# Decoding float64 weights in two steps with the low word rounded on ScalarE, and eleven joint units

## The chip, the cores and the metric

The kernel runs on one core of a Trainium2 chip. The metric is the device time of one execution in microseconds; lower is better. It is compared as the median of several executions. A core has five engines with queues of their own: PE (TensorE, matmul), DVE (VectorE), ACT (ScalarE), POOL (GpSimd) and SP (SyncE, which here issues all the DMAs).

## The reference

Chunked attention with memory tokens, and behind it a mixer with a low-rank token part and a feed-forward part. Batch 4, 8 heads, 768 tokens, head size 64; the model width is 512, the hidden width 2048, the rank 32.

```python
for c in range(nc):                      # chunks of 32 tokens, context 16 left, 8 right, 8 memory tokens
    scores = scale * np.matmul(q_c, k_full.transpose(0, 1, 3, 2))
    a = np.exp(scores - np.max(scores, axis=-1, keepdims=True))
    a = a / (np.sum(a, axis=-1, keepdims=True) + 1e-09)
    out[:, :, c_start:c_end] = np.matmul(a, v_full)
...
h = x.transpose(0, 2, 1) @ U @ V
u = x + h.transpose(0, 2, 1)
ch = np.maximum(u @ w_ch1, 0.0) @ w_ch2
return (u + ch).astype(np.float32)
```

U, V, w_ch1 and w_ch2 come as float64 (the random draws are scaled by a float64 factor), so each weight is two 32-bit words in memory. The kernel has to make numbers of them on the chip.

## The kernel before, in words

**Decoding.** A weight's upper word (sign, exponent, 20 bits of fraction) and lower word lie side by side. The class `Words` (L174) works on a chunk of 128 partitions x 512 numbers, each in three methods and a beginning. `begin` (L189, the instruction is recorded at L194) has ScalarE multiply the upper word, read as a float32, by 2^-112, which shifts the exponent to its place after the next step. `bits` (L199) has VectorE shift the result left by three (L201) and put the sign back (L202): that is the float32 of the upper 20 bits, its last three bits zero. `low` (L206) masks out the exponent (L208) and multiplies it by the lower word and 2^-52 (L211), both on VectorE. `join` (L216, L218) adds the two as floats. A chunk has one raw piece or two, and `begin` and `low` issue one instruction for each piece. Three pairs of work tiles rotate for the chunks in flight (`work_pair`, L156).

**High and low parts.** TensorE multiplies in a reduced precision form of float32, so each product is made of three: high x high, high x low, low x high. `finish` (L313) makes the parts of a chunk: ScalarE casts the joined value to the high part (L330), VectorE subtracts that from it (L331). Low parts of w_ch1 (`w1l`) are saved to HBM (L311) and fetched again for later passes (L379).

**The stream.** w_ch1 and w_ch2 are 16 slices f of 128 hidden columns, so 32 chunks (even ones of w_ch1, odd ones of w_ch2). `stream` (L340) is a generator that decodes them in order, three steps a chunk: in the first the bits of chunk n (and the beginning of chunk n + 1 and the finish of chunk n - 1), in the second its low word, in the third its join. `advance(k)` takes k steps. Whoever needs slice f runs the stream until `done` has reached 2f + 2. `more_w` (L867) issues the loads of raw words five slices ahead.

**The order of the work.** The attention of batch 0 comes first; a few steps of the stream are set into its end (L761, L766, L770). Then `both_blocks` (L1020) does the feed-forward part of batch 0 while the weights are still being decoded. A block is 384 tokens, a batch has two. A unit is one slice f for one block: `w1_step` (L950, matmuls at L958, 12 of them; then ScalarE's relu L964 and VectorE's low part L965) and `w2_step` (L978, matmuls at L1006 and L1011). For f below SPLIT the units of both blocks alternate ("joint"), so that each decoded slice serves two units; from SPLIT on come the solo units of block 0 (f = SPLIT to 15), then those of block 1. Units are counted by n. In each unit the stream is advanced by RATE steps behind its `w1_step`. From n = 2 x SPLIT - 6 the loads of batch 1's attention begin, and behind n = 2 x SPLIT one piece of that attention (`border`, L1082) stands ahead of each unit's `w1_step` and one behind it; what is left over is done in the last unit (L1063). The pieces are short stretches such as the turning of keys (L501), scores (L558), the reduction and the exponentials (L584, L587), transposes (L620), products with the values (L635). The values of tile 1 go to the buffer that tile 0 used (`v_home`, L454), those of tile 2 into a buffer that serves as decoding workspace before. Batches 1 to 3 then run block by block.

The engines' orders: TensorE and SyncE go by the order of the program throughout. VectorE does so up to n = 2 x SPLIT (`paced.close`, L1040) and ScalarE up to n = 2 (`head.close`, L1037); behind those points a planner with modelled costs sets their orders when the program is built. An engine executes its list strictly in order.

Of the kernel before, what the change touches and what calls it, by code (L numbers as in the profile page):

```python
# [9 lines left out]
F32R = mybir.dt.float32r  # L10
BF16 = mybir.dt.bfloat16
AF = mybir.ActivationFunctionType
ALU = mybir.AluOpType
AX = mybir.AxisListType
PSUM = bass.MemoryType.PSUM
I32 = mybir.dt.int32
U32 = mybir.dt.uint32
# [3 lines left out]
NVE = 1  # L21
# [10 lines left out]
WLO = 4  # L32
HIGH = 400
LEAD = 1
SPLIT = 10
EARLY = 5
NDEC = 3
RATE = 3
AHEAD = 2
SOON = 6  # L40
RATEL = 3
# [4 lines left out]
def chunk_attn_then_mixer_kernel(  # L46
# [13 lines left out]
    nc = tc.nc  # L60
    ctx.enter_context(tc.manual_schedule(engines={mybir.EngineType.SP}))
    P = 128
# [3 lines left out]
    CH, DF = w1.shape  # L66
# [3 lines left out]
    w2 = w2.bitcast(I32)  # L70
# [85 lines left out]
    def work_pair():  # L156
        if front[0]:
            f = LASTF - NDEC + ndec[0] % NDEC
            ndec[0] += 1
            both = const.tile([P, 2, 512], F32, name="dec", tag=f"w2_{f}")  # L160
            return both[:, 0, :], both[:, 1, :]
        n = ndec[0] - 2 + nkd[0]
        nkd[0] += 1
        if n < 2 * LASTF - 1:
            home = (vbs[2], vbs[2], vbs[1])[n % 3]
            at = (0, 1024, 0)[n % 3]
        elif n % 3:
            home, at = vbs[1], 1024 * (n % 3 - 1)
        else:
            return slot([P, 512], F32, "dec"), slot([P, 512], F32, "dec")  # L170
        home = home.rearrange("c i d -> c (i d)")[:, at:at + 1024]
        return home[:, 0:512], home[:, 512:1024]

    class Words:  # L174


        def __init__(self, raws, adder, p=P):
            self.raws, self.adder, self.p = raws, adder, p
            self.n = sum(raw.shape[1] for raw in raws)
            self.y = None  # L180

# [22 lines left out]
            )  # L204

        def low(self):  # L206
            yi, ti = (a.bitcast(I32)[0:self.p, 0:self.n] for a in (self.y, self.t))
            nc.vector.tensor_scalar(out=yi, in0=ti, scalar1=-2 ** 23, scalar2=None, op0=ALU.bitwise_and)  # L208
            for raw, c in self.pieces():
                y = self.y[0:self.p, c]  # L210
                nc.vector.scalar_tensor_tensor(  # L211
                    out=y, in0=raw.bitcast(U32)[0:self.p, :, 0], scalar=2.0 ** -52, in1=y,
                    op0=ALU.mult, op1=ALU.mult,
                )

        def join(self):  # L216
            t, y = self.t[0:self.p, 0:self.n], self.y[0:self.p, 0:self.n]
            self.adder.tensor_tensor(out=t, in0=t, in1=y, op=ALU.add)  # L218
            return self.t

    uarea = const.tile([P, 6 * NT * R], F32, name="uarea", tag="ul")
# [2 lines left out]
    VG = 3  # L224
# [83 lines left out]
    def save_w1l():  # L308
        while unsaved:
            f, w1l = unsaved.pop(0)  # L310
            nc.sync.dma_start(out=w1l_d[f].bitcast(F32), in_=w1l.bitcast(F32))  # L311

    def finish(f, which, val):  # L313
        if which == 0:
            save_w1l()
            w1h[f] = const.tile([P, NCK, P], F32R, name=f"w1h{f}", tag=f"w1_{f}")
            hi = w1h[f].rearrange("p c n -> p (c n)")
            w1l = wlo.tile([P, NCK, P], F32R, name="w1l")
            lo = w1l.rearrange("p c n -> p (c n)")
            unsaved.append((f, w1l))  # L320
            w1ls[f] = w1l
        else:
            if f < LASTF:
                pair = const.tile([P, 2, CH], F32R, name=f"w2{f}", tag=f"w2_{f}")
            else:
                if f == LASTF:
                    w2p[0] = const.tile([P, 4 * NVE, CH], F32R, name="w2last", tag=f"w2_{f}")
                pair = w2p[0][:, 2 * (f - LASTF):2 * (f - LASTF) + 2, :]
            hi, lo = w2h[f], w2l[f] = pair[:, 0, :], pair[:, 1, :]
        nc.scalar.copy(out=hi, in_=val)  # L330
        nc.vector.tensor_tensor(out=lo, in0=val, in1=hi.bitcast(F32), op=ALU.subtract)  # L331
        done[0] = 2 * f + which + 1

# [1 line left out]

    def chunk(n):
        f, which = n // 2, n % 2
        return Words(staged[f][which], nc.vector)

    def stream():  # L340

        while 0 not in staged:
            yield
        ahead, before = chunk(0), None
        ahead.begin()
        yield
        for n in range(2 * NF):
            words = ahead
            if n + 1 < 2 * NF and (n + 1) // 2 in staged:
                ahead = chunk(n + 1)  # L350
                ahead.begin()
            else:
                ahead = None
            words.bits()
            if before is not None:
                finish(*before)
            yield
            words.low()
            yield
            before = (n // 2, n % 2, words.join())  # L360
            yield
            if n + 1 < 2 * NF and ahead is None:
                while (n + 1) // 2 not in staged:
                    yield
                ahead = chunk(n + 1)
                ahead.begin()
        finish(*before)
        yield

    weights = stream()  # L370

# [10 lines left out]
    def attention(b, xs):  # L382
# [283 lines left out]
        if b == 0:  # L666
# [40 lines left out]
                k_part(1, h)  # L707
            regroup(qraw, qn, "qn", 1)
            regroup(kraw, kn, "kn", 2)
            u_words = Words([uraw], nc.vector)  # L710
            v_words = Words([vraw], nc.vector, 32 * VG)
            gp.append(ps_o.tile([P, 512], F32, name="acc2"))
            yield
            keep_clock(GAP[0])
# [470 lines left out]
```

## Time and profile before

| what | us |
|---|---|
| median of 3 runs | 699.23 (698.71 to 700.57) |
| the profiled execution | 701.68 |
| its span, first to last instruction | 699.9 |
| TensorE busy in it | 660.4 |
| VectorE / ScalarE busy | 281.1 / 221.3 |

Mean granted clock of TensorE: 0.980 of full speed. In the lines of the profile "a<-b" is the written and the read tile, "x12" a count, and a bracket or the last column is the time that the engine stood idle before, and who ended the wait. Work tiles of the decoding bear the names of the buffers that they borrow (`dec`, `vb`, `vbe`); raw words are `rw` and `raw`.

### The profile page before, as it was taken

What the parts mean: (1) busy time and instruction counts of PE and PEld (TensorE: products, weight loads), DVE (VectorE), ACT (ScalarE), POOL (GpSimd) and SP (SyncE); (2) the same over time, 40 slices, a digit from 0 to 9 for tenths busy, and PEclk for the clock granted to TensorE, in tenths of its full rate; (3) what the DMA queues carried; (4) which work ended last, traced back from release to release, by engine and by line L of the source; (5) the groups of instructions that cost most, each with busy time, mean ns of one, the idle gap of its engine ahead of it and who ended that gap; (6) DMA issues with size and microseconds to landing.
All of it is one profiled execution on the core that took longest, in us unless ns stands there. A gap on an engine that the chain in (4) does not pass through costs nothing.

```text
span 699.9 us, 15008 instructions
## 1 busy us (share of the span) xinstructions
PE 660.4 (94%) x6284; PEld 578.5 (83%) x6284; DVE 281.1 (40%) x574; ACT 221.3 (32%) x740; POOL 10.1 (1%) x35
## 2 busy tenths in 40 slices
PE   7786999897869999999999999999999999999997
PEld 4455999776757899998987999998997999989996
DVE  5859898899732421123223221123222221122112
ACT  4524334347562212535401212535401211111110
POOL 2100000000000000000000000000000000000000
PEclk9988999999898999999999999999999999999999
DMA  8786444852354076443411186443411142214211
GB/s 231 173 262 240 149 153 122 216 138 65 108 140 111 15 227 147 102 108 106 107 59 48 31 231 142 110 100 111 102 55 51 31 136 60 61 31 137 69 51 45
DMA packets 123141, 80.14 MB, mean 115 GB/s; under 512 B 87010, under 2 KB 102498, under 8 KB 123074
## 3 DMA queue, kind: packets, MB, share of 16 engines
q1 hardware_dynamic: 123074, 79.19, 40.7%
q8 instruction: 49, 0.80, 0.5%
q14 instruction: 18, 0.15, 0.1%
HBM read 67.50 MB, written 10.49 MB: 111 GB/s over the span
## 4 chain that ended last, share of the span: by engine, by line
PE 85%; DVE 8%; DMA 3%; issue 2%; ACT 1%; SPq 1%; POOL 0%; DVEq 0%; ACTq 0%; POOLq 0%
PE ps_h L958 36%; PE acc L1006 22%; PE acc L1011 11%; PE ps_a L635 2%; PE ps_a L501 2%; PE ps_a L558 2%; PE acc L655 1%; PE ps_a L942 1%; PE ps_a L1006 1%; PE ps_a L620 1%; DMA vb<-in_v_dram 1%; PE ps_a L661 1%; DVE x L972 1%; DMA raw<-in_moe_w_ch_dram 1%; DMA kraw<-in_k_dram 1%
## 5 line engine op out<-in xcount | busy, mean ns | idle before, releaser
L958 PE MATMUL ps_h<-uh,w1h 128*128 128x384 f32 x508 | 176.7, 349 | 15.0 <-ACT w1h L330 13.2
L965 DVE SCALAR_TENSOR_TENSOR hl<-ps_h,hh 128x384 fp32r<-128x384 f32 x127 | 70.7, 557 | 291.8 <-ACT hh L964 291.8
L958 PE MATMUL ps_h<-ul,w1h 128*128 128x384 f32 x508 | 172.6, 341 | 0.0
L1006 PE MATMUL acc<-w,hh 128*128 128x512 f32 x612 | 159.4, 395 | 0.2 <-issue 0.2
L964 ACT ACTIVATE hh<-ps_h 128x384 fp32r<-128x384 f32 x127 | 63.4, 499 | 300.5 <-PE ps_h L958 300.4
L1006 PEld LDWEIGHTS acc<-w,hh 128*128 128x128 f32 x612 | 112.5, 188 | 24.1 <-issue 2.5
L958 PEld LDWEIGHTS ps_h<-uh,w1h 128*128 128x128 f32 x508 | 96.8, 191 | 17.9 <-ACT w1h L330 14.1
L958 PE MATMUL ps_h<-uh,w1l 128*128 128x384 f32 x508 | 110.6, 339 | 0.4 <-issue 0.4
L958 PEld LDWEIGHTS ps_h<-ul,w1h 128*128 128x128 f32 x508 | 97.1, 191 | 4.1 <-issue 2.3
L958 PEld LDWEIGHTS ps_h<-uh,w1l 128*128 128x128 f32 x508 | 91.4, 191 | 1.1 <-issue 0.7
L1011 PE MATMUL acc<-w,hl 128*128 128x512 f32 x306 | 86.5, 391 | 0.0
L1011 PEld LDWEIGHTS acc<-w,hl 128*128 128x128 f32 x306 | 57.5, 188 | 12.9 <-issue 0.4
L587 ACT ACTIVATE pt<-ps_a,mx 128x64 f32<-128x64 f32 x144 | 43.2, 351 | 13.6 <-DVE mx L584 13.6
L587 ACT ACTIVATION_READ_ACCUMULATOR pt<-ps_a,mx 128x1 f32 x144 | 35.1, 244 | 0.0
L522 ACT COPY kall<-ps_a 128x256 f32<-128x256 f32 x40 | 16.9, 423 | 29.2 <-PE ps_a L501 29.2
L972 DVE TENSOR_TENSOR x<-acc,x 128x512 f32<-128x512 f32 x24 | 15.2, 681 | 20.5 <-PE acc L1011 16.7
L1006 PE MATMUL acc<-w2last,hh 128*128 128x512 f32 x90 | 23.2, 393 | 0.0
L644 DVE TENSOR_TENSOR x<-ps_a,rs 128x256 f32<-128x256 f32 x44 | 15.8, 418 | 12.5 <-PE ps_a L635 9.9
L635 PE MATMUL ps_a<-vb,pT 64*32 64x64 f32 x1152 | 15.0, 235 | 5.6 <-DMA vb<-in_v_dram 5.6
L635 PEld LDWEIGHTS ps_a<-vb,pT 64*32 64x32 f32 x1152 | 13.0, 109 | 8.3 <-issue 7.5
L1006 PEld LDWEIGHTS acc<-w2last,hh 128*128 128x128 f32 x90 | 16.7, 188 | 3.8 <-ACT hh L964 0.4
L558 PEld LDWEIGHTS ps_a<-kall,qt 64*32 64x32 f32 x1344 | 16.1, 105 | 4.4 <-issue 4.3
(206 smaller groups left out, 606.8 us busy)
## 6 DMA issues: line engine op xcount, KB each, us to landing
w1l<-w1ld SPq DMA_DIRECT2D x102, 256.0 KB
rw<-in_moe_w_ch_dram SPq DMA_DIRECT2D x14, 512.0 KB
out_dram<-x SPq DMA_DIRECT2D x24, 256.0 KB
vb<-in_v_dram SPq DMA_DIRECT2D x56, 98.0 KB
raw<-in_moe_w_ch_dram SPq DMA_DIRECT2D x20, 256.0 KB
qn<-in_q_dram SPq DMA_DIRECT2D x36, 128.0 KB
rw<-in_moe_w_ch_dram SPq DMA_DIRECT2D x16, 256.0 KB
w1ld<-w1l SPq DMA_DIRECT2D x16, 256.0 KB
```

The source lines that it names most:

```text
L501: nc.tensor.transpose(out=psv[:, p, r, :], in_=half[:, r, 2 * p:2 * p + 2, :].rearrange("n h d -> n (h d)"), identity=ident,)
L522: copy(out=kt[:, p, :, :, m:m + w], in_=psv[:, q_])
L558: nc.tensor.matmul(out=psv[s][CK * i:CK * i + CK, t, p % 2, p // 2, :], lhsT=qt[p // 2][rows, p % 2, NI * t + i, :], rhs=kall[rows, NB * ( ...
L587: nc.scalar.activation(out=ptv[:, a], in_=sc[:, a], func=AF.Exp, bias=mx[:, a:a + 1], scale=-1.0, accum_out=rs[:, t, g, k_, s:s + 1],)
L635: nc.tensor.matmul(out=psv[g][CK * i:CK * i + CK, t, j], lhsT=pt[j % 2][rows, 2 * t + j // 2, CK * i:CK * i + CK], rhs=vt[rows, NI * t + i ...
L644: nc.vector.tensor_tensor(out=x[:, 4 * D * g:4 * D * g + 4 * D].rearrange("n (j d) -> n j d", d=D), in0=psv[g][:, t], in1=rs[:, t, g].rear ...
L958: nc.tensor.matmul(out=ph[:, :TOK], lhsT=w[:, c, :], rhs=u[c], start=(m == 0), stop=(m + 1 == len(parts)),)
L964: nc.scalar.activation(out=hh, in_=ph[:, :TOK], func=AF.Relu)
L965: nc.vector.scalar_tensor_tensor(out=hl, in0=ph[:, :TOK], scalar=0.0, in1=hh.bitcast(F32), op0=ALU.max, op1=ALU.subtract,)
L972: nc.vector.tensor_tensor(out=x, in0=bank, in1=x, op=ALU.add)
L1006: nc.tensor.matmul(out=acc[tt], lhsT=h[:, sl], rhs=w, start=(begins and m == 0), stop=False,)
L1011: nc.tensor.matmul(out=acc[tt], lhsT=hl[:, sl], rhs=w2h[f], start=False, stop=ends is not None)
```

## The change

The lower word is no longer scaled by the exponent on VectorE. ScalarE multiplies it by 2^-29 and writes it as a whole number (0 to 8), and `join` adds that to the bits of the upper word as an int32: the last three bits are filled, with a carry where needed. So `low` has no instruction on VectorE any more and one per piece on ScalarE. The cast to the high part is taken from the value before the join, and right behind `low`; the subtraction still uses the joined value. The stream has two steps a chunk: beginning of n + 1, bits, low and cast of chunk n; then join and subtraction of chunk n - 1. RATE goes from 3 to 2, SPLIT from 10 to 11, and the rotation of work tiles behind chunk 27 is renumbered, since one chunk more is begun within the front.

```diff
-SPLIT = 10
+SPLIT = 11
...
-RATE = 3
+RATE = 2
...
-        elif n % 3:
-            home, at = vbs[1], 1024 * (n % 3 - 1)
+        elif n % 3 != 1:
+            home, at = vbs[1], 1024 * (n % 3 == 0)
...
         def low(self):
+            for raw, c in self.pieces():
+                nc.scalar.activation(
+                    out=self.y.bitcast(I32)[0:self.p, c], in_=raw.bitcast(U32)[0:self.p, :, 0], func=AF.Copy,
+                    scale=2.0 ** -29,
+                )
+
+        def join(self):
             yi, ti = (a.bitcast(I32)[0:self.p, 0:self.n] for a in (self.y, self.t))
-            nc.vector.tensor_scalar(out=yi, in0=ti, scalar1=-2 ** 23, scalar2=None, op0=ALU.bitwise_and)
-            for raw, c in self.pieces():
-                y = self.y[0:self.p, c]
-                nc.vector.scalar_tensor_tensor(
-                    out=y, in0=raw.bitcast(U32)[0:self.p, :, 0], scalar=2.0 ** -52, in1=y,
-                    op0=ALU.mult, op1=ALU.mult,
-                )
-
-        def join(self):
-            t, y = self.t[0:self.p, 0:self.n], self.y[0:self.p, 0:self.n]
-            self.adder.tensor_tensor(out=t, in0=t, in1=y, op=ALU.add)
+            nc.vector.tensor_tensor(out=ti, in0=ti, in1=yi, op=ALU.add)
             return self.t
...
     def finish(f, which, val):
...
-        nc.scalar.copy(out=hi, in_=val)
         nc.vector.tensor_tensor(out=lo, in0=val, in1=hi.bitcast(F32), op=ALU.subtract)
...
+        for n in range(2 * NF + 1):
+            if n < 2 * NF:
+                while n not in begun:
+                    start(n)
+                    if n not in begun:
+                        yield
+                start(n + 1)
+                begun[n].bits()
+                begun[n].low()
+                nc.scalar.copy(out=homes(n // 2, n % 2), in_=begun[n].t)
+                yield
+            if n > 0:
+                finish((n - 1) // 2, (n - 1) % 2, begun[n - 1].join())
+                yield
```

The new function `homes` only allocates the tiles of the parts, which `finish` did before; `start(n)` begins chunk n once, if its raw words have been asked for.

More of the change, by code (lines that the diff above doesn't have):

```diff
@@ L174, in chunk_attn_then_mixer_kernel, with __init__ @@
     class Words:
-        def __init__(self, raws, adder, p=P):
-            self.raws, self.adder, self.p = raws, adder, p
+        def __init__(self, raws, p=P):
+            self.raws, self.p = raws, p
             self.n = sum(raw.shape[1] for raw in raws)
@@ L206, in low @@
         def low(self):
[L207 to L208 removed]
             for raw, c in self.pieces():
[L210 to L213 removed]
+                nc.scalar.activation(
+                    out=self.y.bitcast(I32)[0:self.p, c], in_=raw.bitcast(U32)[0:self.p, :, 0], func=AF.Copy,
+                    scale=2.0 ** -29,
                 )
         def join(self):
[L217 to L218 removed]
+            yi, ti = (a.bitcast(I32)[0:self.p, 0:self.n] for a in (self.y, self.t))
+            nc.vector.tensor_tensor(out=ti, in0=ti, in1=yi, op=ALU.add)
             return self.t
@@ L311, in save_w1l, with homes @@
             nc.sync.dma_start(out=w1l_d[f].bitcast(F32), in_=w1l.bitcast(F32))
+    def homes(f, which):
+        if which == 0:
+            w1h[f] = const.tile([P, NCK, P], F32R, name=f"w1h{f}", tag=f"w1_{f}")
+            return w1h[f].rearrange("p c n -> p (c n)")
+        if f < LASTF:
+            pair = const.tile([P, 2, CH], F32R, name=f"w2{f}", tag=f"w2_{f}")
+        else:
+            if f == LASTF:
+                w2p[0] = const.tile([P, 4 * NVE, CH], F32R, name="w2last", tag=f"w2_{f}")
+            pair = w2p[0][:, 2 * (f - LASTF):2 * (f - LASTF) + 2, :]
+        w2h[f], w2l[f] = pair[:, 0, :], pair[:, 1, :]
+        return w2h[f]
     def finish(f, which, val):
@@ L315, in finish @@
             save_w1l()
-            w1h[f] = const.tile([P, NCK, P], F32R, name=f"w1h{f}", tag=f"w1_{f}")
             hi = w1h[f].rearrange("p c n -> p (c n)")
             w1l = wlo.tile([P, NCK, P], F32R, name="w1l")
-            lo = w1l.rearrange("p c n -> p (c n)")
             unsaved.append((f, w1l))
             w1ls[f] = w1l
+            lo = w1l.rearrange("p c n -> p (c n)")
         else:
[L323 to L330, printed above, removed]
+            hi, lo = w2h[f], w2l[f]
         nc.vector.tensor_tensor(out=lo, in0=val, in1=hi.bitcast(F32), op=ALU.subtract)
@@ L337, in chunk, with start @@
         f, which = n // 2, n % 2
-        return Words(staged[f][which], nc.vector)
+        return Words(staged[f][which])
     def stream():
+        def start(n):
+            if n < 2 * NF and n // 2 in staged and n not in begun:
+                begun[n] = chunk(n)
+                begun[n].begin()
+        begun = {}
         while 0 not in staged:
             yield
-        ahead, before = chunk(0), None
-        ahead.begin()
+        start(0)
         yield
[L347 to L368, printed above, removed]
+        for n in range(2 * NF + 1):
[12 more added lines that the diff above has]
+                yield
     weights = stream()
@@ L709, in attention @@
             regroup(kraw, kn, "kn", 2)
-            u_words = Words([uraw], nc.vector)
-            v_words = Words([vraw], nc.vector, 32 * VG)
+            u_words = Words([uraw])
+            v_words = Words([vraw], 32 * VG)
             gp.append(ps_o.tile([P, 512], F32, name="acc2"))
```

## The prediction

> **What bounds the kernel now.** I read the page first, then TensorE's list of waits, then two windows, then TensorE's timeline around its gaps. The page and the waits:
>
> ```profile
> span 699.9 us, 15008 instructions
> ## 1 busy us (share of the span) xinstructions
> PE 660.4 (94%) x6284; PEld 578.5 (83%) x6284; DVE 281.1 (40%) x574; ACT 221.3 (32%) x740; POOL 10.1 (1%) x35
> ```
>
> ```profile
> PE ps_h L958 <- ACT w1h L330: 13.2, 3, 6.5
> PE ps_a L635 <- DMA vb<-in_v_dram: 5.6, 1, 5.6
> ```
>
> TensorE has work for 94% of the span. The change adds or removes no matmul, it only orders some of them otherwise, so the whole effect must be in TensorE's idle time and in stretches where its clock is low. Two windows (columns: window, length, then busy time of PE, PEld, DVE, ACT, POOL, then granted clock, DMA share, GB/s) say where that is not and where it is:
>
> ```profile
> 144.80:246.83 102.03, 86.90 (x1156) 73.91 (x1155) 60.95 (x128) 48.08 (x189) 2.02 (x6) 0.93 0.33 86
> 75.17:133.40 58.23, 58.23 (x296) 53.03 (x295) 51.73 (x100) 22.86 (x47) 0.00 (x0) 1.00 0.55 168
> ```
>
> The second row is seven pairs of joint units (n = 3 to 16). TensorE is never idle there: a pair takes 58.23 / 7 = 8.32 us whatever the decoding costs, and VectorE needs 51.73 / 7 = 7.39 us of it. So no time is to be won there, although VectorE looks almost full. The first row runs from unit 19 to the end of batch 0: TensorE is idle for 102.03 - 86.90 = 15.13 us, with the clock at 0.93. TensorE's timeline has the long gaps in brackets, each in front of the matmul that waited:
>
> ```profile
> 62.25 1.65 PE L958 MATMUL ps_h<-uh,w1h 128*128 128x384 f32 x4 [6.48 <-ACT w1h L330]
> ...
> 136.38 0.44 PE L958 MATMUL ps_h<-uh,w1h 128*128 128x384 f32 x1 [2.23 <-ACT w1h L330]
> ...
> 167.70 1.48 PE L558 MATMUL ps_a<-kall,qt 64*32 64x64 f32 x128
> 173.71 0.69 PE L958 MATMUL ps_h<-uh,w1h 128*128 128x384 f32 x1 [4.54 <-ACT w1h L330]
> ...
> 210.82 2.46 PE L635 MATMUL ps_a<-vb,pT 64*32 64x64 f32 x126 [5.63 <-DMA vb<-in_v_dram]
> ```
>
> Three of them wait for a decoded weight, the last for values of batch 1. Behind the long ones the clock is low; the chain of waits shows the same twelve matmuls (one L958 unit of one block) at two speeds:
>
> ```profile
> 173.71 4.21 PE ps_h L958 x12
> ...
> 213.28 3.86 PE ps_h L958 x12
> ...
> 239.29 2.11 PE ps_h L958 x12
> ```
>
> So the gaps before 173.71 and 210.82 cost a further 4.21 - 2.11 = 2.10 and 3.86 - 2.11 = 1.75 us, and the one before 62.25, whose first four matmuls took 1.65 us, about as much as the former, 2.10. The gap of 2.23 us left no such stretch: the first matmul behind it took 0.44 us, the one behind 4.54 took 0.69.
>
> **What the step costs, per chunk.** VectorE's groups, then ScalarE's (mean ns behind the busy time):
>
> ```profile
> L218 DVE TENSOR_TENSOR vbe<-vbe 128x512 f32<-128x512 f32 x16 | 11.1, 693 | 0.4
> L202 DVE SCALAR_TENSOR_TENSOR vbe<-vbe 128x512 int32<-128x512 int32 x16 | 11.1, 693 | 0.5
> ...
> L201 DVE TENSOR_SCALAR vbe<-vbe 128x512 int32<-128x512 int32 x16 | 6.7, 421 | 0.0
> L208 DVE TENSOR_SCALAR vbe<-vbe 128x512 int32<-128x512 int32 x16 | 6.7, 420 | 0.0
> L211 DVE SCALAR_TENSOR_TENSOR vbe<-rw,vbe 128x512 f32<-128x512 uint32 x8 | 5.5, 693 | 0.2
> L331 DVE TENSOR_TENSOR w<-vbe,w 128x512 fp32r<-128x512 f32 x8 | 5.5, 692 | 1.8 <-ACT w L330 1.8
> ```
>
> ```profile
> L330 ACT CAST w1h<-vbe 128x512 fp32r<-128x512 f32 x8 | 5.0, 624 | 6.9 <-DVE vbe L218 6.9
> L194 ACT ACTIVATE vbe<-rw 128x512 f32<-128x512 f32 x7 | 4.7, 675 | 0.0
> L194 ACT ACTIVATE vb<-raw 128x256 f32<-128x256 f32 x9 | 4.0, 449 | 4.3 <-DMA raw<-in_moe_w_ch_dram 4.3
> ```
>
> Before, a chunk is 0.42 + 0.69 (L201, L202) + 0.42 (L208) + 0.69 (L211) + 0.69 (L218) + 0.69 (L331) = 3.61 us on VectorE and 0.68 + 0.62 = 1.30 on ScalarE. After, L208 and L211 are gone: 2.50 on VectorE, and ScalarE has one more pass over the raw words, 0.68 in one piece or 2 x 0.45 in two: 1.98 to 2.2. The integer add is not in the trace; its bounds are 0.42 (one source, L201) and twice 0.69; I take the 0.69 of L202, which also reads two int32 sources. The new ScalarE pass with a whole-number output is not there either; bounds 0.62 (L330) and 0.90 (two pieces), I take L194's, which reads the same strided words. As important: the cast to the high part now needs only L201 and L202, not the join, so what TensorE waits for first is ready about 0.42 + 0.69 + 0.69 = 1.8 us sooner in its chunk.
>
> A rule of the Trainium skill speaks against this move: "ScalarE: Activation LUTs", Rules for kernel authors, wants adds and multiplications on VectorE, which it calls up to about three times faster per element in bf16. Here the rows say 675 against 693 ns for the same 128x512, since VectorE's form read two sources in fp32, so I go by the rows. By the rule the pass would take some 2.1 us (an estimate, three times 0.69), 1.4 us more for each chunk; that is a case of the last rival.
>
> **Joint units** (RATE 3 to 2, three steps to two): before and after, the program finishes one chunk per unit, n + 3 before unit n. TensorE's 8.32 us per pair stays above VectorE's (7.39 less about 1.9) and ScalarE's (22.86 / 7 = 3.3 plus about 1.5). Gain nil. SPLIT 11 adds one more such pair and takes one solo unit from each block: at the change to solo units 25 of 32 chunks are finished in program order instead of 23.
>
> **Unit 1 (62.25).** Before: 6.48 idle and 2.10 slow, 8.58. Its first four matmuls need only the high part of chunk 2, which now is there; the next four need the low part. VectorE ends unit 0's input here:
>
> ```profile
> 54.70 1.01 DVE L932 TENSOR_TENSOR ul<-ps_a,uh 128x384 fp32r<-128x384 f32 x2
> ```
>
> So it is free at 55.71, and behind that its program has join and subtraction of chunk 1, one L965 (about 0.56), two bit operations of chunk 3, join and subtraction of chunk 2: 4 x 0.69 + 0.56 + 1.11 = 4.4. New in front of it: low word and cast of chunk 2 now stand on ScalarE before the cast of the gate (L843), because that engine goes by program order there; between 0 and 0.90 + 0.62 = 1.5 late, I take 0.8. The low part is then ready at 55.7 + 0.8 + 4.4 = 60.9; TensorE has done unit 0 (56.5) and four matmuls (0.7), so it is idle for 3.7. That is nearer to the gap of 4.54, which made the clock fall, than to 2.23, which did not: two thirds of 2.10, 1.4, more. The skill's "TensorE: Matmul & The Clock Gate", What's actually happening, sets the fall after an idle window of about 3.4 us; the four gaps of this trace agree, and by it the 3.7 is over the line. New cost 0.8 + 3.7 + 1.4 = 5.9; gain 2.7.
>
> **136.38: 2.2 gained.** ScalarE's timeline has the cause:
>
> ```profile
> 134.75 0.43 ACT L194 ACTIVATE vb<-raw 128x256 f32<-128x256 f32 x1 [4.13 <-DMA raw<-in_moe_w_ch_dram]
> ```
>
> The planner, free at n = 20 to order VectorE as well, put the first pass of a late chunk ahead of the cast that TensorE needed, and its DMA wasn't there. Two units later that word has landed. If the planner errs alike elsewhere, up to 2.2 is lost again.
>
> **173.71: what is late next.** 4.54 + 2.10 = 6.64 were paid; with seven chunks left and 2.5 instead of 3.6 each, I keep 1.5 (0 to 4.54). But that gap hid something: the scores turned at 167.70 are reduced and exponentiated before the next piece, their transposes, can run.
>
> ```profile
> 172.30 1.26 DVE L584 TENSOR_REDUCE mx<-ps_a 128x8 f32<-128x512 f32 x2
> ```
>
> ```profile
> 173.56 0.31 ACT L587 ACTIVATE pt<-ps_a,mx 128x64 f32<-128x64 f32 x1
> ...
> 178.13 0.28 ACT L587 ACTIVATION_READ_ACCUMULATOR pt<-ps_a,mx 128x1 f32 x1
> ```
>
> One reduction (0.63) and the exponentials (178.41 - 173.56 = 4.85) make 5.5, and one unit (2.11) covers part of it: at the most 3.4 comes back. The first tile half's transposes can run before the second half is exponentiated, so I take 3.0. Net gain 6.64 - 1.5 - 3.0 = 2.1.
>
> **210.82: 7.4 gained, 4.1 given back.** SyncE issues the values in order, behind block 0's outputs:
>
> ```profile
> 201.03 1.53 SPq L974 DMA_DIRECT2D out_dram<-x  x3
> ...
> 205.09 2.97 SPq L482 DMA_DIRECT2D vb<-in_v_dram  x4
> ```
>
> From the outputs to the last landing (210.82) it takes 9.8 us, and TensorE wanted the values at 210.82 - 5.63 = 205.2. Block 0 ended at n = 25 and the piece that needs them stood at n = 27. With one joint pair more, block 0 ends at n = 26 and the piece stands at n = 29. Between them lie three half units (3 x 2.11) and four pieces of batch 1. A piece is at the most (86.90 - 13 x 4.16) / 20 = 1.6, with the slow stretches and the closing transposes in it; I take 1.25 as an estimate, so 11.3 us of TensorE work against 9.8. Gain 5.63 + 1.75 = 7.4. The same shift takes block 0's final products from between scores and transposes of the second tile: 5.5 against one unit and one piece, 0 to 3.4 idle, I take 2.0. And the pieces of batch 1 now have nine solo units instead of eleven, so the last of them come in a row behind the last unit: six adds of 512 on VectorE at 0.69 (as L331) are 4.1, half of it covered: 2.1 idle. Net 7.4 - 2.0 - 2.1 = 3.3. The other idle time of the window, 15.13 - 4.54 - 5.63 = 5.0, I leave.
>
> **Sum:** 2.7 + 2.2 + 2.1 + 3.3 = 10.3 us. The profiled execution took 701.68 (span 699.9 and 1.8 around it) and would take 691.4. The median of the runs shown is 699.23, 2.45 below it, so 688.9.
>
> **The rivals.**
> - *Nothing comes back:* exponentials and adds stay covered and the late chunks are in time: 3.0 + 1.5 + 2.0 + 2.1 less, 680.3. For it: VectorE and ScalarE are free sooner everywhere. Against: 4.85 us of exponentials behind a unit of 2.11.
> - *The chain takes the load's place, no change:* each chunk now goes VectorE, ScalarE, VectorE. If they don't overlap it takes 1.11 + 0.68 + 0.62 + 0.69 + 0.69 = 3.8, two a solo unit 7.6, with L964/L965 8.7, against about 6.7 of TensorE work (4.16 and two pieces at 1.25). Four units at 2.0 are 8, with two slow stretches (4.2) 12.2, against the gain before that of 11.8: 699.6. It decides from 6.7 us per unit. For it: ScalarE is order-bound. Against: three chunks have homes, so neighbours can overlap.
> - *Slower:* the same chain, and the planner sets one group of exponentials (4.85) ahead of a cast or an L964 that TensorE needs: 699.6 + 4.9 = 704.5. It decides once ScalarE's queue at units 23 to 26 is over 6.7 us; by the row of the window (48.08 in 102.03) it is half empty.
> - *It doesn't lighten the load, the new operations are dear:* an integer add at twice 0.69, seven chunks x 0.69 = 4.9 dearer, 693.8; or a ScalarE pass at three times 0.69, 2.1 instead of 0.68, for the eight chunks of the solo units 11.2, 700.1. Against the latter: L194 reads the same strided words at 0.68.
>
> **How the numbers follow.** Chances: forecast 0.60 (684 to 694), nothing comes back 0.18, no change 0.10, slower 0.06, dear add 0.04, dear pass 0.02. The range 679 to 696 leaves out the slower case, the dear pass, most of no change and the end of the first rival, 0.19. About 0.3% (2 us) is what can be told from no change. Faster: 0.60 + 0.18 + 0.04 + 0.04 (of no change) = 0.86; same 0.06 + 0.02 = 0.08; slower 0.06.
>
> **What would show it.** Right: L208 and L211 gone, a second L194-like ScalarE line at 0.4 to 0.7 us, an int32 add at 0.69; seven or eight pairs still 8.3 us apart; unit 1's gap in front of w1l, not w1h, at 3 to 4 us; no wait for values at L635; new gaps in front of L620. Wrong: waits for w1h of over 5 us after the joint units, ScalarE over 0.8 busy for 20 us there, or an add far from 0.69.

## The result, and the profile after

| what | before | after |
|---|---|---|
| median of 4 runs each, us | 699.90 (698.71 to 702.65) | 690.13 (688.84 to 691.22) |
| ratio, 95% interval | | 0.9854 (0.9817 to 0.9891) |
| the profiled execution / its span | 701.68 / 699.9 | 689.29 / 687.5 |
| clock of TensorE granted, mean | 0.980 | 0.990 |

The change makes the kernel 9.8 us faster by the medians and 12.4 by the two profiled spans. A second measurement of the same two kernels (below, the last experiment) gave 692.14 against 700.00, so 8 to 10 us is what the change is worth.

The page of the kernel after, its span and its engines:

```profile
span 687.5 us, 14945 instructions
...
PE 658.2 (96%) x6284; PEld 576.0 (84%) x6284; DVE 246.7 (36%) x488; ACT 241.9 (35%) x792; POOL 10.1 (1%) x35
```

TensorE has the same 6284 matmuls and nearly the same busy time (660.4 before). VectorE has lost 34 us, ScalarE gained 21. So what is saved must again be looked for in TensorE's idle time. Its list of waits (total, times, longest) no longer has a wait for `w1h` or for values:

```profile
PE ps_a L500 <- DMA qn<-in_q_dram: 3.5, 2, 3.0
PE ps_h L957 <- DVE w1l L333: 3.4, 1, 3.4
...
PE ps_a L619 <- ACT pt L586: 2.0, 6, 0.6
...
PE ps_a L634 <- ACT pt L586: 1.1, 1, 1.1
```

The decoding's groups, by form (mean ns behind the busy time):

```profile
L202 DVE SCALAR_TENSOR_TENSOR vbe<-vbe 128x512 int32<-128x512 int32 x15 | 10.4, 691 | 0.4
L215 DVE CUSTOM_DVE_ANT_0 vbe<-vbe 128x1024 uint16<-128x1024 uint16 x15 | 10.3, 685 | 0.0
...
L194 ACT ACTIVATE vbe<-rw 128x512 f32<-128x512 f32 x7 | 4.7, 670 | 0.0
L208 ACT ACTIVATE vbe<-rw 128x512 int32<-128x512 uint32 x7 | 4.6, 662 | 0.0
```

L208 is now the lower word on ScalarE: 0.66 us, like the upper word's pass beside it (0.67). L215 is the integer add. It stands under another name than its source, as a custom operation on the two 16-bit halves of each word, and takes 0.685 us, as much as L202.

**Where the time came from.** It helps to cut the span at two marks that both kernels have: the first joint pair behind unit 1 (the first line of 24 matmuls in the chain of waits, at 75.33 before and 71.07 after) and the first matmuls of batch 1's feed-forward part (246.83 and 234.89). In front of the first mark the kernel after is 75.33 - 71.07 = 4.26 us ahead, between the marks it gains 7.68 more, and behind them 0.46: together the 12.4. The windows between the marks, before and then after (window, length, busy time of PE, PEld, DVE, ACT, POOL, then clock, DMA share, GB/s):

```profile
75.33:246.83 171.50, 154.14 (x1494) 134.74 (x1494) 121.31 (x246) 74.92 (x245) 2.02 (x6) 0.96 0.43 122
```

```profile
71.07:234.89 163.82, 154.22 (x1494) 132.92 (x1494) 93.33 (x176) 89.14 (x280) 2.02 (x6) 0.98 0.44 123
71.07:129.30 58.23, 58.23 (x296) 52.99 (x296) 40.88 (x73) 32.41 (x70) 0.00 (x0) 1.00 0.50 158
```

TensorE's busy time is the same to 0.1 us, so all 7.68 are idle time: 17.36 before, 9.60 after. The second row of the kernel after is seven joint pairs: 58.23 us, to the hundredth what they took before, though VectorE has 40.88 instead of 51.73 in them. In the joint units nothing was to be won and nothing was.

TensorE's timeline between the marks has the 9.6 us in small pieces. The longest, in order (idle time in the bracket):

```profile
172.47 0.33 PE L619 MATMUL ps_a<-ident,pt 128*128 128x128 f32 x1 [0.26 <-ACT pt L586]
...
174.63 0.33 PE L619 MATMUL ps_a<-ident,pt 128*128 128x128 f32 x1 [0.65 <-ACT pt L586]
...
175.82 0.33 PE L619 MATMUL ps_a<-ident,pt 128*128 128x128 f32 x1 [0.27 <-ACT pt L586]
175.90 2.31 PE L1005 MATMUL acc<-w,hh 128*128 128x512 f32 x6
...
184.04 1.63 PE L1005 MATMUL acc<-w2last,hh 128*128 128x512 f32 x6
...
195.21 0.55 PE L500 MATMUL ps_a<-ident,qn 128*128 128x128 f32 x3 [2.98 <-DMA qn<-in_q_dram]
...
206.75 1.54 PE L634 MATMUL ps_a<-vb,pT 64*32 64x64 f32 x126 [1.05 <-ACT pt L586]
```

The first three rows stand for six of one step of batch 1, the transposes of tile 0. ScalarE is still exponentiating, so each transpose waits for its own piece, 0.26 to 0.65 us. Behind them the clock is low: six matmuls at L1005 take 2.31 us, where 1.63 is usual, and the clock granted between 160 and 180 us is 0.92. Then the queries of tile 2 are missing for 3 us. SyncE's queue says why:

```profile
188.70 3.01 SPq L973 DMA_DIRECT2D out_dram<-x  x3
...
192.24 1.54 SPq L406 DMA_DIRECT2D qn<-in_q_dram  x3
```

Three of the query loads stand behind block 0's outputs, as the values did before.

**Unit 1.** In front of the first mark, the place that the prediction spoke of:

```profile
54.83 0.86 PE L957 MATMUL ps_h<-uh,w1h 128*128 128x384 f32 x4
59.07 0.97 PE L957 MATMUL ps_h<-uh,w1l 128*128 128x384 f32 x4 [3.39 <-DVE w1l L333]
```

The high part is there at once, the low part is waited for, 3.39 us. VectorE works without a break up to it, from the join of chunk 1 to the subtraction of chunk 2:

```profile
54.75 0.68 DVE L215 CUSTOM_DVE_ANT_0 dec<-dec 128x1024 uint16<-128x1024 uint16 x1
...
58.33 0.69 DVE L333 TENSOR_TENSOR w1l<-dec,w1h 128x512 fp32r<-128x512 f32 x1
```

Not all of the 4.26 us is unit 1's. The last products of the low-rank part before it (L655 before, L654 after) already began 2.1 us earlier, at 46.23 instead of 48.31:

```profile
48.31 1.96 PE L655 MATMUL acc<-x,uarea 128*96 128x512 f32 x4 [0.86 <-DVE x L644]
```

```profile
46.23 1.96 PE L654 MATMUL acc<-x,uarea 128*96 128x512 f32 x4 [0.86 <-DVE x L643]
```

From there to the first mark it is 27.02 us before and 24.84 after: 2.2 us belong to unit 1 in these two traces. The six traces below whose kernels have the same front as the kernel after take 23.68 to 25.14 for that stretch, so unit 1 is worth 1.9 to 3.3 us. The other 2.1 lie where this start differs from execution to execution, whatever the kernel: in the same six traces it lies between 45.20 and 49.40 (last section).

### The profile page after: what moved, and what is told of

Its sections match the earlier page's. It is cut to its first block, busy times and chain, and to the rows that moved or that the text cites. A ratio compares the mean times of both kernels' runs of the same rounds, so it can differ in the third digit from the quotient of the medians.

```text
span 687.5 us, 14945 instructions
## 1 busy us (share of the span) xinstructions
PE 658.2 (96%) x6284; PEld 576.0 (84%) x6284; DVE 246.7 (36%) x488; ACT 241.9 (35%) x792; POOL 10.1 (1%) x35
## 4 chain that ended last, share of the span: by engine, by line
PE 86%; SPq 6%; DMA 2%; DVE 2%; ACT 2%; issue 1%; ACTq 0%; DVEq 0%
PE ps_h L957 38%; PE acc L1005 23%; PE acc L1010 12%; SPq L481 3%; PE ps_a L500 2%; PE ps_a L634 2%; PE ps_a L1005 2%; PE ps_a L557 2%; PE ps_a L941 1%; ACT pt L586 1%; PE ps_a L619 1%; PE ps_a L1010 1%; DMA rw<-in_moe_w_ch_dram 1%; PE ps_a L660 1%; DMA vb<-in_v_dram 1%
## 5 line engine op out<-in xcount | busy, mean ns | idle before, releaser
L957 PE MATMUL ps_h<-uh,w1h 128*128 128x384 f32 x508 | 174.7, 345 | 0.5 <-issue 0.5
L1005 PE MATMUL acc<-w,hh 128*128 128x512 f32 x606 | 158.4, 397 | 0.0
L1005 PEld LDWEIGHTS acc<-w,hh 128*128 128x128 f32 x606 | 111.8, 188 | 24.2 <-issue 2.5
L957 PE MATMUL ps_h<-uh,w1l 128*128 128x384 f32 x508 | 108.7, 334 | 3.4 <-DVE w1l L333 3.4
L957 PEld LDWEIGHTS ps_h<-uh,w1l 128*128 128x128 f32 x508 | 89.8, 188 | 3.7 <-DVE w1l L333 3.7
L1005 PE MATMUL acc<-w2last,hh 128*128 128x512 f32 x90 | 23.1, 392 | 0.0
L1005 PEld LDWEIGHTS acc<-w2last,hh 128*128 128x128 f32 x90 | 16.8, 188 | 3.4
L557 PE MATMUL ps_a<-kall,qt 64*32 64x64 f32 x1344 | 18.5, 225 | 0.2 <-issue 0.2
L1005 PE MATMUL ps_a<-w,hh 128*128 128x512 f32 x66 | 17.0, 393 | 0.0
```

What stands on the lines that cost most here:

```text
L557: nc.tensor.matmul(out=psv[s][CK * i:CK * i + CK, t, p % 2, p // 2, :], lhsT=qt[p // 2][rows, p % 2, NI * t + i, :], rhs=kall[rows, NB * ( ...
L957: nc.tensor.matmul(out=ph[:, :TOK], lhsT=w[:, c, :], rhs=u[c], start=(m == 0), stop=(m + 1 == len(parts)),)
L1005: nc.tensor.matmul(out=acc[tt], lhsT=h[:, sl], rhs=w, start=(begins and m == 0), stop=False,)
```

## The experiments

The theory behind them: 7.7 us come from VectorE's lighter load in the last chunks (no weight is late any more), 2.2 from unit 1, and what is left is batch 1's attention. Rivals: the other order (early cast, two steps) does it, not the load; the eleventh joint pair does it; ScalarE's longer chain holds the rest back. Each run was timed beside the kernel before on the same chip, which took 700.11 us beside the first four, 701.40 beside the next four and 700.00 beside the last four; the ratios are to these. The column "stage" is the time between the two marks; the three columns behind it are busy times in it, all four from one trace of each kernel.

| kernel | median, us | ratio to before (95%) | stage | TensorE | VectorE | ScalarE |
|---|---|---|---|---|---|---|
| before | 699.90 | | 171.50 | 154.14 | 121.31 | 74.92 |
| after | 690.13 | 0.9854 (0.9817 to 0.9891) | 163.82 | 154.22 | 93.33 | 89.14 |
| after, ten pairs | 692.39 | 0.9894 (0.9826 to 0.9963) | 163.99 | 153.35 | 93.38 | 87.72 |
| before, eleven pairs | 704.58 | 1.0066 (1.0032 to 1.0101) | 175.57 | 159.96 | 121.06 | 75.77 |
| after, low word on VectorE | 699.41 | 0.9988 (0.9959 to 1.0017) | 168.08 | 155.43 | 121.58 | 75.78 |
| after, late cast | 694.49 | 0.9920 (0.9886 to 0.9953) | 164.00 | 154.29 | 94.37 | 90.60 |
| after, chunk 3 begun later | 692.14 | 0.9889 (0.9835 to 0.9943) | 163.52 | 153.95 | 93.54 | 88.93 |
| after, four loads a unit | 690.00 | 0.9859 (0.9815 to 0.9902) | 161.55 | 153.74 | 93.23 | 88.73 |
| after, keys between | 687.27 | 0.9841 (0.9770 to 0.9912) | 159.20 | 150.24 | 93.30 | 88.69 |
| after, the last three together | 687.02 | 0.9825 (0.9764 to 0.9887) | 162.18 | 154.05 | 93.42 | 88.75 |
| keys between and four loads | 687.37 | 0.9824 (0.9779 to 0.9869) | 160.12 | 151.66 | 93.25 | 88.87 |
| after, low word twice | 691.08 | 0.9874 (0.9843 to 0.9905) | 162.77 | 152.65 | 93.91 | 105.11 |
| keys between, ten pairs | 689.72 | 0.9838 (0.9798 to 0.9878) | 162.37 | 151.95 | 93.50 | 87.93 |
| after again | 692.14 | 0.9880 (0.9844 to 0.9916) | 163.73 | 154.25 | 93.33 | 88.92 |

### Ten joint pairs with the new decoding

```diff
-SPLIT = 11
+SPLIT = 10
```

> The changed kernel with ten joint pairs as before. Theory of the three places (unit 1, the decoding left over for the solo units, and the place of block 0's end among the pieces of batch 1): the 4 us of the front and the 2.2 us before the last joint pair stay won, nine chunks are left over instead of seven, the wait for the values of batch 1 is back at 3 to 6 us and the wait for its queries (3.5 us) is gone: 690 to 695 us, nearest 692. Rival that VectorE's lighter load is all: the number of pairs doesn't matter, 690. Rival that the eleventh pair is all: 698 to 700.

Measured: the stage is that of the kernel after, 163.99 against 163.82, and the medians cannot be told apart. The wait for values is back, nearly as long as in the kernel before, and the wait for queries is gone:

```profile
198.51 2.52 PE L634 MATMUL ps_a<-vb,pT 64*32 64x64 f32 x126 [5.17 <-DMA vb<-in_v_dram]
```

With eleven pairs the kernel after pays for queries (2.98 and 0.47), for values nothing, and for more small waits; with ten it pays 5.17 for values. The shift moves the loss from one load to another. It is not the source of the gain.

### Eleven joint pairs with the old decoding

```diff
-SPLIT = 10
+SPLIT = 11
```

> The kernel before with eleven joint pairs, decoding untouched. Three places: the gap before unit 1 stays 6.5 us, the wait for the values goes, one for the queries of tile 2 comes in its place, seven chunks are left at 3.6 us each and the waits for weights behind the joint units are 0 to 5 us: 693 to 698 us. Rival that VectorE's load is all: 700. Rival that the eleventh pair is all: 690.

Measured: slower than the kernel before by 0.7%, where a gain was expected. The values are in time, as foreseen, but weights are late at four places, one of them unit 1 in front of the stage, and queries and exponentials are late as well. The idle time of the stage is no longer for that: 15.61 us against 17.36 before. What rises is TensorE's busy time, from 154.14 to 159.96, though the work is the same: the clock is low behind the weight at 167, behind the transposes that are fed one by one (six matmuls at L1006 take 2.91 us there) and behind the queries.

```profile
63.11 1.65 PE L958 MATMUL ps_h<-uh,w1h 128*128 128x384 f32 x4 [6.48 <-ACT w1h L330]
135.40 0.44 PE L958 MATMUL ps_h<-uh,w1h 128*128 128x384 f32 x1 [0.49 <-ACT w1h L330]
145.11 0.44 PE L958 MATMUL ps_h<-uh,w1h 128*128 128x384 f32 x1 [1.16 <-ACT w1h L330]
...
167.74 0.69 PE L958 MATMUL ps_h<-uh,w1h 128*128 128x384 f32 x1 [2.20 <-ACT w1h L330]
...
191.25 2.91 PE L1006 MATMUL acc<-w,hh 128*128 128x512 f32 x6
...
211.39 1.88 PE L501 MATMUL ps_a<-ident,qn 128*128 128x128 f32 x7 [3.01 <-DMA qn<-in_q_dram]
```

So the eleventh pair is a loss with the old decoding and worth nothing with the new one as it stands. Two of the late weights lie inside the joint pairs, at 135 and 145. The first has the cause of the gap at 136.38 in the kernel before: in ScalarE's order the first pass of a later chunk, whose raw words have not landed, stands ahead of the cast.

```profile
134.41 0.43 ACT L194 ACTIVATE vb<-raw 128x256 f32<-128x256 f32 x1 [3.03 <-DMA raw<-in_moe_w_ch_dram]
134.74 0.60 ACT L330 CAST w1h<-vbe 128x512 fp32r<-128x512 f32 x1
```

For the second, ScalarE's cast waits for VectorE, which is busy for 24.20 of the 25.69 us from 134.31 to 160. That its 3.6 us a chunk are what makes it late there was not tested by itself.

### The new order with the lower word on VectorE

Two steps, early cast, eleven pairs; only the decoding's `low` and `join` are those of before.

```diff
         def low(self):
+            yi, ti = (a.bitcast(I32)[0:self.p, 0:self.n] for a in (self.y, self.t))
+            nc.vector.tensor_scalar(out=yi, in0=ti, scalar1=-2 ** 23, scalar2=None, op0=ALU.bitwise_and)
             for raw, c in self.pieces():
-                nc.scalar.activation(
...
+                nc.vector.scalar_tensor_tensor(
+                    out=y, in0=raw.bitcast(U32)[0:self.p, :, 0], scalar=2.0 ** -52, in1=y,
...
```

> The changed order (two steps, cast to the high part before the join, eleven pairs) with the low word back on VectorE as a float product and a float add: VectorE pays 3.6 us a chunk again. Three places: the low part for unit 1 comes some 1.5 to 2.5 us later, so that gap is 5 to 6 us, and the joint pairs still take 8.3 us; behind them 1.1 us more for each of seven chunks, partly hidden: 691 to 695. Rival that VectorE's load is all: 699 to 700. Rival that only the order counts: 690.

Measured: no gain over the kernel before can be seen in the medians. The waits for a high part have turned into waits for a low part:

```profile
PE ps_h L960 <- DVE w1l L336: 8.0, 4, 4.7
PE ps_a L503 <- DMA qn<-in_q_dram: 3.2, 1, 3.2
```

The four stand in unit 1 (4.67) and around the end of the joint pairs (0.52, 1.13 and 1.67). The time is the one that the rival named which credits the load alone, and my theory, which gave the order 4 to 8 us over the kernel before, missed it: with an early cast TensorE gets its high parts, and then waits for low parts from the same VectorE.

But the rival does not follow from this run. It differs from the kernel before in two things, order and split, and the run above shows that the split by itself costs 4.5 us with this decoding. Beside that run, the order (two steps, early cast) is the only difference: 699.41 against 704.58, with ratios whose intervals do not meet (0.9959 to 1.0017 and 1.0032 to 1.0101), so there the order gains some 5 us. The stages say it too: 175.57 with the old order, 168.08 with the new one, which is 3.4 below the kernel before as well, a gain that its medians do not show. The load is then worth the step from here to the kernel after, 7 to 9 us by the medians, and 4.3 in the stage (168.08 to 163.82). The lighter load in the old order was not run.

### The cast late again, the rest of the kernel after

```diff
     def finish(f, which, val):
...
+        nc.scalar.copy(out=homes(f, which), in_=val)
         nc.vector.tensor_tensor(out=lo, in0=val, in1=hi.bitcast(F32), op=ALU.subtract)
...
-                nc.scalar.copy(out=homes(n // 2, n % 2), in_=begun[n].t)
```

> The changed kernel with the cast to the high part back behind the join (the low word stays on ScalarE). Three places: at unit 1 TensorE waits for the high part again, which is then as late as the low part but for one subtraction; the gap is 4 to 5 us and the clock falls for the whole unit; the solo units lose 0 to 3 us: 691 to 695. Rival that VectorE's load is all: 690.

Measured: as expected. The stage is unchanged (164.00), the median 2.4 to 4.4 us above the two of the kernel after, and the one wait that comes back is unit 1's:

```profile
60.48 1.65 PE L957 MATMUL ps_h<-uh,w1h 128*128 128x384 f32 x4 [4.77 <-ACT w1h L324]
```

With the lighter load the early cast matters in unit 1 alone. From the low-rank products to the first mark this kernel takes 26.06 us, against 27.02 before and 23.68 to 25.14 with the front of the kernel after: in single traces the early cast gives 0.9 to 2.4 of unit 1's gain, and the lighter VectorE with the rest of the order about 1.0.

### Chunk 3 begun later, so that the gate is not held up

In the kernel after, ScalarE begins chunk 3 in front of the gate's cast, and its raw words are not there:

```profile
48.30 0.67 ACT L194 ACTIVATE dec<-rw 128x512 f32<-128x512 f32 x1 [1.96 <-DMA rw<-in_moe_w_ch_dram]
...
50.04 0.36 ACT L842 CAST g<-acc 96x256 fp32r<-96x256 f32 x1
```

The products that the gate needs ended at 46.23 + 1.96 = 48.19, so it is 1.85 late.

```diff
-                start(n + 1)
+                if n != 2:
+                    start(n + 1)
```

> The changed kernel, but the beginning of chunk 3 is taken out of the step ahead of the gate and stands in the next step. Theory that the gate's cast is late because ScalarE, bound to its order there, waits for chunk 3's raw words: from the last L654 group to the gate's cast 1.0 us or less instead of 1.85, and 0.5 to 1.5 us off the total: 688.5 to 689.5 against 690. Rival that the low word and the cast of chunk 2 are what holds the gate: no change, 690.

Measured: the gate is 0.91 late instead of 1.85, and no gain can be seen in the median; from the low-rank products to the first mark it is 25.11 us, inside the 23.68 to 25.14 of the other traces. Half of the gate's delay comes from the new ScalarE passes and stays. This run does not settle what the other half costs.

### Four loads a unit instead of three

```diff
-RATEL = 3
+RATEL = 4
```

> The changed kernel with four instead of three steps of batch 1's loads per unit. Theory that the queries of tile 2 wait behind block 0's outputs in SyncE's order: the 3.0 and 0.5 us before them go, with the slow stretch behind them; the transposes of the second tile then wait about 2 us for their exponentials: 1 to 4 us off, 686 to 689. Rival that DMA bandwidth or free buffers hold the queries: no change, 690.

Measured: the queries are in time and the wait for them is gone; the transposes behind them wait 2.09 instead, as expected. The stage is 2.3 us shorter, yet the median is that of the kernel after. In the profiled execution the front had started later by about as much (73.08 for the first mark), so the gain of the stage stands (1.8 of it are idle time) and that of the whole is not shown by this run.

```profile
197.09 1.77 PE L619 MATMUL ps_a<-ident,pt 128*128 128x128 f32 x8 [2.09 <-ACT pt L586]
```

### The turning of tile 2's keys moved between scores and transposes of tile 0

```diff
             s_part(0)
             yield
+            need("kn", 2)
+            for h in two:
+                k_part(2, h)
+            yield
             for s in two:
                 t_part(0, s)
...
-            need("kn", 2)
-            for h in two:
-                k_part(2, h)
-            yield
```

> The changed kernel with one piece moved: the keys of tile 2 are turned between the scores of tile 0 and their transposes, so the exponentials have a unit and a piece more to run under. Theory that the transposes at 172 wait for exponentials only: they take 1.0 us instead of 4.4 and the clock doesn't fall behind them: 3 to 5 us off, 685 to 687. Rival that ScalarE's queue is what is short, so that the wait moves to the next reader: under 1 us off, 689 to 690.

Measured: the stage falls by 4.6 us to 159.20 and the median to 687.27. Of the 4.6 only 0.6 are idle time (9.60 to 8.96), 4.0 are TensorE's busy time, that is clock. Two waits are shortened by the one move: the transposes now wait 1.56 in one piece instead of 1.97 in six (the keys ahead of them wait 0.72) and the clock stays up behind them, and the queries' loads get ahead of the outputs in SyncE's queue, since the buffers of the keys come free earlier:

```profile
171.69 2.93 SPq L406 DMA_DIRECT2D qn<-in_q_dram  x3
188.17 2.82 SPq L973 DMA_DIRECT2D out_dram<-x  x3
```

```profile
179.31 0.66 PE L619 MATMUL ps_a<-ident,pt 128*128 128x128 f32 x4 [1.56 <-ACT kall L525]
...
195.31 1.23 PE L619 MATMUL ps_a<-ident,pt 128*128 128x128 f32 x8 [2.09 <-ACT pt L586]
```

That the buffers come free earlier is read from the order in the queue; no run tested it by itself. The last row is luck in part: in the next two kernels the clock fell behind this same wait.

### The three together, and two of them

> The last three edits together. If the waits are independent the gains add: 5 to 9 us off 690, 681 to 685. If removing one uncovers another (exponentials of tile 1, values of tile 1): 685 to 688.

> The keys' piece moved between scores and transposes, and the loads behind the outputs spread one unit later (RATEL 4), without the later beginning of chunk 3. If the two edits of batch 1's attention act on different waits, the stretch from unit 1's end to the end of batch 0 is 1 to 2 us shorter than with the keys' piece alone (159.2) and the time 685 to 687. If both only clear the same wait (the queries behind the outputs), the stretch is 159 to 162 and the time 686 to 688, as with one of them.

The last expectation has the sense of RATEL 4 the wrong way round: the loads are asked for sooner, four a unit. Measured: the gains do not add. With the keys' piece moved, the queries are already in time, and the four loads clear nothing more (160.12 against 159.20). All three together have the same waits as the keys' move alone, and their stage is 3 us longer by TensorE's busy time (154.05 against 150.24): there the clock fell behind the same wait of 2.09 us and once more among the closing pieces (twelve matmuls at L942 took 2.57 us, where 1.85 is usual), and it did neither in the run of the keys alone.

```profile
197.53 1.97 PE L620 MATMUL ps_a<-ident,pt 128*128 128x128 f32 x8 [2.09 <-ACT pt L587]
```

Keys and loads against the kernel after, measured together: 687.37 against 692.14. The intervals of their ratios, 0.9779 to 0.9869 and 0.9844 to 0.9916, overlap by a little; the four versions with the keys' piece moved have medians of 687.0 to 689.7, the kernel after 690.1 and 692.1. I take the moved piece as a gain of 3 to 5 us, and this as the version to keep; the three stages with eleven pairs, 159.20 to 162.18, put it at 1.6 to 4.6, and the intervals do not prove it.

### The lower word twice

```diff
-            for raw, c in self.pieces():
+            for raw, c in 2 * list(self.pieces()):
                 nc.scalar.activation(
```

The second pass writes the same numbers again.

> The low word's ScalarE pass issued twice a chunk (the second writes the same numbers again): 0.66 to 0.88 us more ScalarE work for each of 32 chunks, 21 to 28 us in all. If ScalarE has slack beside TensorE everywhere but at unit 1, only unit 1's wait and the front grow, by 1 to 2 us: 690 to 693. If the chain through ScalarE sets the pace of the last chunks, as the no-change and the dear-pass cases of the prediction have it, waits for w1h come back in the solo units, 0.7 to 1.4 us for each chunk there: 695 to 701.

Measured: 691.08, between the two medians of the kernel after, and a stage of 162.77, not above 163.82:

```profile
72.89:235.66 162.77, 152.65 (x1495) 131.97 (x1494) 93.91 (x176) 105.11 (x321) 2.02 (x6) 0.99 0.44 124
```

ScalarE did 16 us more in the stage (105.11 against 89.14) and TensorE did not wait for a weight once in it; in unit 1 it waited 3.38, for 3.39 in the kernel after. So the longer chain over ScalarE holds nothing back there, and the cases of the prediction that lived on it (a chain that takes the load's place, a dear pass) are a long way off.

### Ten pairs with the keys' piece moved

> The kernel after with the keys' piece moved and ten joint pairs instead of eleven. If the shift to eleven pairs only trades the wait for values against the waits for queries and exponentials, then with those two cleared eleven is better by what ten still waits for the values (5.2 us and some slow clock), and this kernel takes 690 to 693. If ten and eleven are equal in any case, it takes 686 to 688.

Measured: 689.72 and a stage of 162.37, in between what the two theories expected, against 687.37 and 160.12 with eleven pairs and four loads (which by the run before change nothing here). Its longest wait at the values is for the exponentials, one of 3.03 more stands before the turning of keys:

```profile
196.16 0.47 PE L634 MATMUL ps_a<-vb,pT 64*32 64x64 f32 x16 [3.46 <-ACT pt L586]
```

In idle time the stage has 10.42 us with ten pairs and 8.13 to 8.96 in the three traces with eleven, so the eleventh pair may be worth 1.5 to 2.3 us once queries and exponentials do not eat it up. As a whole the three stages, 159.20 to 162.18, differ more by their clock than that, and the medians, with intervals 0.008 to 0.009 wide in the ratio, do not prove it.

### The kernel after again

> The kernel after, unchanged, beside the versions above on the same chip: 688.5 to 691.5. If the kernel with the moved keys' piece is really better, the one with both edits is 2 to 4 us below it in this call; if that was the chip, they are level.

Measured: 692.14, slightly above what was expected, with a stage of 163.73 against 163.82. The stage repeats to 0.1 us in these two traces; the front (72.48 for the first mark instead of 71.07) does not.

## Why the prediction was right, and where its steps were not

The time came out as forecast, 690.1 for 688.9, and the whole was the forecast case: 10.3 us expected, 9.8 by the medians. That it came so close is luck in part, since two errors of 4 us cancelled. The steps in order:

- **The costs of a chunk.** Right. The add takes 0.685 (0.69 taken), the new ScalarE pass 0.66 (0.68 taken), both bounds were wider than needed.
- **Joint units, gain nil.** Right for the pairs: 58.23 for seven, as before. VectorE fell from 51.73 to 40.88, 1.55 a pair where 1.9 was put. By the forecast's own 1.11 a chunk it would be 2.2, since a pair decodes two chunks; the two windows don't hold quite the same work (14 bit operations at L202 before, 15 after), which makes the 1.55 too small.
- **Unit 1, gain 2.7.** Right in kind and nearly in size. In front of `w1l` as forecast, 3.39 idle for 3.7; the list of VectorE up to the low part took 54.75 to 59.02, 4.3 for 4.4. The gate was 1.85 late instead of 0.8, because the beginning of chunk 3 waited for its raw words ahead of it, an instruction that the prediction had not counted among those moved past the gate; without it, it was 0.91 late. The gain from the low-rank products on is 2.2 in these two traces, 1.9 to 3.3 over all of them.
- **136.38 and 173.71, 2.2 and 2.1.** The forecast kept 1.5 us of late weights; there is none. The rows to hold beside it are the runs with the load on VectorE: with 3.6 us a chunk and eleven pairs, weights behind unit 1 are late by 3 to 4 us in sum, whatever the order of the steps. With 2.5 they never were. That is not all VectorE's doing: at 136.38, as the prediction says, ScalarE stood before raw words, and in the kernel after its passes at 133 and 134 still wait for theirs (0.85 and 0.24 us), but TensorE does not wait for a weight behind them. The exponentials came back as foreseen (3.0 taken), at the place named: the transposes at L619 are fed one by one and the eight of them stretch from 171.77 to 175.9, 4.1 us, against the 1.0 that eight take elsewhere.
- **210.82, 3.3 by the shift of the split.** This is the step that failed. The wait for values went, but the step was credited to the eleventh pair as a gain of its own, and that it is not: ten and eleven pairs give the same stage (163.99 and 163.82). The forecast looked at SyncE's queue for the values and stopped there; it did not ask what else the shift would bring behind block 0's outputs. That was the queries of tile 2, 3.45 us of wait and a low clock behind. For the closing pieces 2.1 were put; their waits at L860 are under 1 us in all.
- **Two errors cancelled, by luck.** Of the idle time between the marks, the gaps of 2.23 + 4.54 + 5.63 = 12.40 are gone, and 7.76 net were won, so 4.6 came back, where the sum had 1.5 + 3.0 + 2.0 + 2.1 = 8.6. On the other side the sum had 2.10 + 1.75 = 3.85 us of low clock saved there, and nothing was saved: TensorE's busy time is the same, 154.14 and 154.22. New gaps, at 172 to 176 and at 195, slow the matmuls behind them as the old ones did. So 4.0 too many were put back and 3.85 too many taken out.

Of the rivals, "no change" and "slower" rested on the chain over ScalarE at units 23 to 26. The run with the lower word doubled speaks against both by measurement. Two products in the last rival are off: seven times 0.69 is 4.8, not 4.9, and the dear pass was counted for eight chunks where seven are left, 9.8 for 11.2; neither condition was met (0.685 for the add, 0.66 for the pass). "Nothing comes back" was wrong by the waits named above. That the change lightens VectorE is needed for the gain: with the lower word back on VectorE and all else as in the kernel after, the medians show none. It is not all of it: with eleven pairs and the old load the new order alone takes the time from 704.58 to 699.41, about what the eleventh pair costs there.

The trace of before gave a hint of what the eleventh pair costs with the old decoding: a chunk needs 3.61 us of VectorE, and two of them, with what else VectorE does, 7.39 in 8.32 of TensorE. "So no time is to be won there" was true, but a share of 0.89 leaves little reserve for one more pair in strict order. How much of the loss is due to that stays open, since the first of the late weights waited for raw words.

## What to carry to other kernels

When a load hides behind another (the values behind the outputs), and an edit moves the place where they meet, list everything that is queued behind the same outputs, for the wait passes to the next of them. A gap that is removed takes its slow clock with it only if no new gap of some 2 to 3 us, and no row of short ones, opens; sum idle time and TensorE's busy time separately, since errors in them hide each other. And an edit that has several parts (order, load, split) should be taken apart on the chip even when the total is as forecast: here the split alone made the old kernel some 4.5 us slower, the order on top of it gained 5, and the load on top of both 7 to 9. The parts depend on each other, so a run that adds one part last does not show that the others do nothing.

## What the runs showed of the hardware that was not expected

**A start that wanders.** At 37 to 41 us, among the products with the values of batch 0 (L634, L635 in the kernels with another line more), TensorE stands idle before one matmul, and the profile has no releaser for it ("issue"). The row in the kernel before, the kernel after, and the three edits together:

```profile
38.23 0.21 PE L635 MATMUL ps_h<-vb,pt 64*32 64x64 f32 x1 [1.63 <-issue]
```

```profile
37.71 0.21 PE L634 MATMUL ps_h<-vb,pt 64*32 64x64 f32 x1 [0.68 <-issue]
```

```profile
40.41 0.26 PE L635 MATMUL ps_h<-vb,pt 64*32 64x64 f32 x1 [5.62 <-issue]
```

The products are the same in all three; only the decoding beside them differs. But the kernel after itself had 0.68 in one execution and 2.28 in the other. The first mark moves with it, and this is about as much as the executions of one kernel differ (688.84 to 691.22, 687.97 to 694.67). What TensorE waits for there was not found; it is why the stage and not the whole time was compared above.

**The same gap, two clocks.** A wait of 2.09 us at the same transposes left the eight behind it at 1.23 us in one execution, 1.77 and 1.97 in two others (rows above; 1.03 is usual), and one of 3.36 to 3.39 in unit 1 left the first four matmuls at 0.97 in two traces and 1.51 to 1.65 in eight. The Trainium skill ("TensorE: Matmul & The Clock Gate", What's actually happening) has the clock follow a window of about 3.4 us that runs freely and doesn't start with the kernel's work, so that the point of the change varies. The runs agree with that as far as they go: gaps of 2 to 3.4 us are where the outcome differs; the window itself is in no row here. The six waits of 0.26 to 0.65 us at L619, none of them long, were also followed by slow matmuls (2.31 for 1.63), so it is not the longest gap alone that counts.
